# A fused window attention and GELU layer: identity and mask built on chip, first queries pre-scaled, and every engine's order written into the kernel

## The chip, the cores and the metric

The kernel runs on one core of one Trainium2 chip. A core has TensorE (PE; its weight loads are shown as PEld), VectorE (DVE), ScalarE (ACT), GpSimd (POOL) and SyncE (SP), each with its own stream of instructions in a fixed order; they meet at semaphores only. POOL and SP also issue DMAs. The metric is the device time of one execution in microseconds (us), lower is better.

## The reference

Streaming attention over 4 batches, 8 heads, 768 positions, 64 per head: each query sees the 128 latest keys and the first 4 ("sinks"). Its output, as 3072 tokens of 512, goes through two matrices with a quick GELU between them.

```python
scores = scale * np.matmul(q, k.transpose(0, 1, 3, 2))
rel = pos[:, None] - pos[None, :]
keep = is_sink | ((rel >= 0) & (rel < int(window)))
scores = np.where(keep, scores, -1000000000.0)
a = np.exp(scores - np.max(scores, axis=-1, keepdims=True))
a = a / (np.sum(a, axis=-1, keepdims=True) + 1e-09)
x = np.matmul(a, v)            # as tokens x 512
h = x @ w_in                   # 512 x 2048
g = h * (1.0 / (1.0 + np.exp(-1.702 * h)))
out = g @ w_out                # 2048 x 512
```

## The kernel before, in words

The 3072 tokens are 24 blocks of 128, six to a batch. `ORD` puts the first block of each batch (0, 6, 12, 18) at the front, since these see no earlier block; two blocks in this order make a group, 12 in all. The work of one block:

- POOL loads q, k and v in 16 bits (`load_block`, L369 and L378) into `qkn` and `v65`. Block 0's q and k come in 32 bits through the SP and ACT queues (L316) and are cast on chip (L374 to L376, recorded at the copy helper's L351).
- q and k are transposed to `qkT`: for the first 8 blocks in `ORD` on TensorE with an identity (`tq`, L471; copied out of PSUM at L347 or L351, the two lines of `copy` for VectorE and ScalarE), for the others by a DMA transpose on SP (L490).
- Scores: own block (`own`), the block before (`prv`), the sinks (`misc`), L524, L549 and L568; these matmuls use 64 of the array's 128 rows. For the four first blocks a mask is added by a matmul with a bf16 identity (`masks`, L516) before the scores; for the others VectorE picks own or previous scores by a predicate (L592).
- Softmax: VectorE takes maxima (L604), subtracts (L659), ScalarE takes the exponent (L692). For the first four blocks the second half goes straight through ScalarE with the negated, scaled maximum `nb` as bias (L635, L645).
- The weights are transposed, on TensorE for the first four blocks (`ta`, L755), by DMA for the others (L793), after which POOL's two selects split own and previous keys (L698, L704).
- Values (`av`, L814 to L824) with a column of ones for the sum, normalisation on VectorE (L835, L836) into `xn`, its transpose `xT` (L849 on TensorE for eight blocks, L862 by DMA).

A group then runs through the layer: eight units of `hT` (L884), the GELU on ScalarE into `gT` (L914), and two output tiles `o`, each in four pieces (L935), copied to `osb` and stored by SP (L953). The weights `w_in` and `w_out` come in four quarters each (L387, L396), in the same POOL queue as the blocks. Exponent and GELU need different tables on ScalarE.

What sets the order: the kernel first records its operations in a `Plan`, each with its engines, its cost, its dependences and the buffers it takes and gives. `Plan.run` then plays a list schedule over them with planned costs, in which every operation has a priority from the written list `KEYS`; where an operation may run on two engines, this decides which. The result is emitted as one fixed order per engine. `fill` matmuls (L975) that compute nothing are put where the plan sees TensorE idle in the first 45 us. `RING` gives the number of buffers of each kind: 3 PSUM banks `mm`, 2 `own`, 2 `pv`, 4 output tiles `osb`.

The loads at the start of SP are the lines L316 to L321: block 0's q, the identity, the mask `bias0`, then small constants.

Of the kernel before, what the change touches and what calls it, by code (L numbers as in the profile page):

```python
# [15 lines left out]
AF = mybir.ActivationFunctionType  # L16
# [15 lines left out]
    tq=(0, 1, 2, 3, 4, 5, 6, 7),  # L32
    ta=(0, 1, 2, 3),
    tx=(0, 1, 2, 3, 4, 5, 6, 7),
    nb={0: 1, 1: 1, 2: 1, 3: 1},
    wide=(1, 3),
    split=(0,),
    gbatch={},
    tanh=(),
    after0=25.0,  # L40
    vsb=15.0,
    slack={'v': 1.0, 's': 1.0, 'x': 1.0, 'e': 0.0, 'p': 0.0},
    merge=8,
    pemask=(0, 1, 2, 3),
    f32=(0,),
    sel2=(),
    fill=(1.5, 45.0, 0.15, 0.11),
    chain=99,
    gap=3,
    steady=8,  # L50
    after=8.0,
# [6 lines left out]
KEYS = [  # L58
    int(x)
    for x in """  # L60
# [32 lines left out]
""".split()  # L93
]
# [15 lines left out]
class Op:  # L110
    def __init__(self, eng, key, cost, emit, deps=(), take=(), give=(), table=None, lat=0.2, xfer=0.0, after=0.0, batch=0, post=0.0, slack=0.0, half=False):
        self.eng = eng if isinstance(eng, dict) else {eng: cost}
        self.key, self.emit = key, emit
        self.deps = [d for d in deps if d is not None]
        self.take, self.give, self.table, self.batch = list(take), list(give), table, batch
        self.lat, self.xfer, self.after, self.post, self.slack, self.half = lat, xfer, after, post, slack, half
        self.on = self.start = None
        self.end = self.done = 1.0e9
        for b in self.give:
            b.left += 1  # L120
# [6 lines left out]
class Plan:  # L127
    TABLE, LANES, ROWS = 1.35, 8, 0.1
    ENGINES = (PE, ACT, DVE, POOL, SP)

    PRE, SHARE = {POOL: 0.6, SP: 0.0}, {POOL: 0.68, SP: 0.32}

    def __init__(self, rings):
        self.ops, self.free, self.blk = [], dict(rings), 0
# [7 lines left out]
    def run(self):  # L142
        inf = 1.0e9
        t_eng = {e: 1.0 for e in self.ENGINES}
        free, table, batch, now, half = dict(self.free), "exp", 0, 0.0, False
        order, gives, events = [], [], [1.0]
        pending = {e: sorted((o for o in self.ops if e in o.eng), key=lambda o: (o.key, o.seq)) for e in self.ENGINES}
        events += [op.after for op in self.ops if op.after > 0.0]
        queue = {POOL: [], SP: []}
        lanes = {POOL: [], SP: []}  # L150
        count = len(self.ops)
        slacks = sorted({op.slack for op in self.ops if op.slack})

        def finish(op):
            events.append(op.done)
            for b in op.give:
                b.left -= 1
                b.t = max(getattr(b, "t", 0.0), op.done)
                if b.left == 0:
                    gives.append((b.t, b.ring))  # L160
                    events.append(b.t)

        while count or any(queue.values()):
            for item in [x for x in gives if x[0] <= now + EPS]:
                gives.remove(item)
                free[item[1]] += 1
            for e in self.ENGINES:
                if t_eng[e] > now + EPS:
                    continue
                for op in pending[e]:  # L170
                    if op.start is not None or op.after > now + EPS:
                        continue
                    if batch and op.table is not None and op.table != table:
                        continue
                    if any((d.end + 0.03 if d.on == e and not d.xfer else d.done + op.slack) > now + EPS for d in op.deps):
                        continue
                    if any(free[r] < n for r, n in op.need().items()):
                        continue
                    if op.xfer and len(lanes[e]) >= self.LANES and lanes[e][-self.LANES].done > now + EPS:
                        continue  # L180
                    break
                else:
                    continue
                cost = op.eng[e]
                if op.table is not None:
                    if op.table != table:
                        cost, table = cost + self.TABLE, op.table
# [824 lines left out]
```

## Time and profile before

| | |
|---|---|
| timed runs | 231.02, 232.11, 234.61 us (median 232.11) |
| profiled execution | 230.8 us |
| its span, first to last instruction | 229.1 us |
| granted TensorE clock | 0.999 |
| busy: TensorE, VectorE, ScalarE, POOL | 220.9, 132.4, 134.0, 110.8 us |
| fill matmuls | 65 of 2257 |
| first matmul that computes something | 5.66 us |
| first maximum on VectorE | 9.57 us |
| first matmul of the layer (hT) | 22.36 us |
| last matmul starts | 225.7 us |

The profile comes from one execution. Its times count from the start of the span. A row of the timeline gives start, busy time, engine, line, operation, output and inputs, the number of instructions, and in brackets the idle time of the engine before it and what ended that. A row of groups has the same names, then busy time and mean duration of one, then idle time before. In the table by windows, each stretch has its length and then the busy time of each engine with the number of its instructions, the granted clock, the DMA engines' share and GB/s. Matmuls overlap in the array, so their cost is the time from one start to the next, not the duration of one.

### The profile page before, as it was taken

How to read it: one execution, taken by the hardware profiler on the slowest of the kernel's cores; microseconds unless marked ns; L12 is line 12 of the kernel's file. 1: busy time of each engine (PE TensorE's matmuls, PEld its weight loads, DVE VectorE, ACT ScalarE, POOL GpSimd, SP SyncE). 2: the span in 40 equal slices, each digit the busy share in tenths (PEclk: the TensorE clock that was granted, in tenths of full speed). 3: DMA queues.
4: the chain of work that ended last, by engine and by line, in shares of the span. 5: the costliest groups of instructions: out<-in, count | busy, mean ns of one | idle time of the engine just before them, and what ended most of it. 6: DMA issues, size and time to landing. Idle time of an engine off the chain costs nothing.

```text
span 229.1 us, 5503 instructions
## 1 busy us (share of the span) xinstructions
PE 220.9 (96%) x2257; PEld 156.4 (68%) x2257; DVE 132.4 (58%) x331; ACT 134.0 (58%) x203; POOL 110.8 (48%) x122
## 2 busy tenths in 40 slices
PE   6998999999899999989999999999999999999994
PEld 3686986844686685676686686685596586685772
DVE  5499264887579177886793776676967830020000
ACT  4598765672766655548556757466467558451631
POOL 8982543906995196186294393397330240300000
PEclk9999999999999999999999999999999999999999
DMA  9999999999999999979999999999942922330202
GB/s 134 153 192 191 200 198 177 155 172 232 195 132 144 198 165 133 185 168 129 187 183 134 186 163 134 189 180 155 219 93 46 106 92 49 97 92 3 92 0 92
DMA packets 132280, 32.89 MB, mean 144 GB/s; under 512 B 124928, under 2 KB 129312, under 8 KB 132256
## 3 DMA queue, kind: packets, MB, share of 16 engines
q0 software_dynamic: 77024, 13.37, 76.3%
q1 hardware_dynamic: 54192, 18.92, 43.5%
q10 hardware_dynamic: 1040, 0.26, 0.5%
q8 instruction: 17, 0.28, 0.5%
q14 instruction: 7, 0.06, 0.1%
HBM read 27.43 MB, written 6.29 MB: 147 GB/s over the span
## 4 chain that ended last, share of the span: by engine, by line
PE 82%; DVE 9%; DMA 5%; issue 1%; ACT 1%; SPq 0%; DVEq 0%; ACTq 0%
PE o L935 34%; PE hT L884 33%; DMA xT<-xn 3%; PE av L820 2%; DVE mx L604 2%; PE own L549 2%; DMA bias<-cbias 2%; DVE xn L836 2%; PE av L824 2%; PE av L814 2%; DVE e L659 2%; PE tq L471 1%; PE prv L549 1%; PE misc L975 1%; DVE own L592 1%
## 5 line engine op out<-in xcount | busy, mean ns | idle before, releaser
L884 PE MATMUL hT<-xT,w_in 128*128 128x256 f16 (+1 forms) x832 | 92.8, 264 | 0.0
L935 PE MATMUL o<-w_out,gT 128*128 128x512 f16 (+1 forms) x400 | 89.9, 371 | 0.0
L914 ACT ACTIVATE gT<-hT 128x512 f16<-128x512 f32 x96 | 56.6, 597 | 45.4 <-PE hT L884 44.9
L884 PEld LDWEIGHTS <-w_in 128*128 128x128 f16 x832 | 74.3, 98 | 12.1 <-DMA xT<-xn 0.2
L935 PEld LDWEIGHTS <-gT 128*128 128x128 f16 x400 | 36.7, 98 | 35.0
L704 POOL TENSOR_SCALAR_AFFINE_SELECT atp<-at 128x1024 f16<-128x1024 f16 x20 | 21.9, 1094 | 71.7 <-DMA at<-a 67.5
L592 DVE COPY_PREDICATED own<-later,prv 128x512 f32<-128x512 uint16 x40 | 25.9, 692 | 25.7 <-PE prv L549 22.7
L604 DVE TENSOR_REDUCE mx<-own 128x4 f32<-128x512 f32 x48 | 30.9, 683 | 0.3 <-PE own L524 0.2
L692 ACT ACTIVATE a<-e 128x1056 f16<-128x1056 f32 (+1 forms) x24 | 23.8, 1007 | 11.3 <-issue 8.7
L659 DVE TENSOR_TENSOR e<-own,mx 128x512 f32<-128x512 f32 x44 | 28.8, 684 | 1.0
L351 ACT COPY osb<-o 128x512 f32<-128x512 f32 (+1 forms) x20 | 11.3, 565 | 25.3 <-PE o L935 20.0
L369 POOL DMA_DIRECT2D v<-in_v_dram x24 | 21.7, 912 | 5.1 <-DMA w_out<-in_moe_w_out_dram 3.3
L378 POOL DMA_DIRECT2D qkn<-in_q_dram x23 | 20.5, 905 | 5.2 <-DMA w_in<-in_moe_w_in_dram 3.1
L378 POOL DMA_DIRECT2D qkn<-in_k_dram x23 | 21.0, 914 | 3.2 <-DMA w_out<-in_moe_w_out_dram 2.1
L698 POOL TENSOR_SCALAR_AFFINE_SELECT at<-at 128x1024 f16<-128x1024 f16 x20 | 21.8, 1091 | 1.4
L835 DVE RECIPROCAL rcp<-av 128x4 f32<-128x4 f32 x48 | 8.4, 176 | 23.7 <-PE av L824 19.5
L836 DVE TENSOR_TENSOR xn<-av,rcp 128x256 f16<-128x256 f32 x48 | 20.4, 425 | 1.7
L820 PE MATMUL av<-v,at 128*128 128x65 f16 x192 | 17.1, 194 | 0.0
L820 PEld LDWEIGHTS <-at 128*128 128x128 f16 x192 | 14.2, 97 | 1.2 <-ACT at L351 0.2
L824 PE MATMUL av<-v,atp 128*128 128x65 f16 x160 | 14.8, 193 | 0.0
L914 ACT ACT_TABLE_LOAD x10 | 12.8, 1283 | 0.2
L975 PE MATMUL misc<-fill 128*128 128x256 f16 x65 | 11.1, 317 | 1.1 <-DVE fill L324 1.1
(56 smaller groups left out, 168.0 us busy)
## 6 DMA issues: line engine op xcount, KB each, us to landing
out_dram<-osb SPq DMA_DIRECT2D x23, 256.0 KB, 2.2
v<-in_v_dram POOLq DMA_DIRECT2D x24, 128.0 KB, 5.7
qkn<-in_k_dram POOLq DMA_DIRECT2D x23, 128.0 KB, 5.7
qkn<-in_q_dram POOLq DMA_DIRECT2D x23, 128.0 KB, 5.6
w_in<-in_moe_w_in_dram POOLq DMA_DIRECT2D x4, 512.0 KB, 10.3
w_out<-in_moe_w_out_dram POOLq DMA_DIRECT2D x4, 512.0 KB, 15.4
at<-a SPq DMA_TRANSPOSE x20, 4.2
rawk<-in_k_dram ACTq DMA_DIRECT2D x1, 256.0 KB, 4.5
```

Source lines behind the costliest of these rows:

```text
L378: key, 0.88, lambda: nc.gpsimd.dma_start(buf()[:, i, w], src), 0.9,
L592: nc.vector.copy_predicated(out=own[l](), mask=later.unsqueeze(1).to_broadcast((P, 4, P)), data=prv[l]())
L604: lambda l=l, own=own, small=small: nc.vector.tensor_reduce(out=small[:, l], in_=own[l](), axis=AX.X, op=ALU.max),
L659: nc.vector.tensor_tensor(out=e32()[:, 512 * l : 512 * l + 512].rearrange("p (j s) -> p j s", j=4), in0=own[l](), in1=small[:, l].unsqueez ...
L692: nc.scalar.activation(out=a16()[:, lo:hi], in_=e32()[:, lo:hi], func=AF.Exp, scale=scale)
L698: nc.gpsimd.affine_select(out=dst()[:, lo : lo + n], in_=at()[:, lo : lo + n], pattern=[[0, n], [1, P]], compare_op=ALU.is_ge, fill=0.0, b ...
L704: nc.gpsimd.affine_select(out=dst()[:, lo : lo + n], in_=at()[:, lo : lo + n], pattern=[[0, n], [-1, P]], compare_op=ALU.is_gt, fill=0.0, ...
L820: nc.tensor.matmul(av()[:, j], ato()[:, c], v65[:, b, h], start=(r == 0), stop=(r == 0))
L836: nc.vector.tensor_tensor(out=xn()[:, i].rearrange("p (j l) d -> p l j d", l=2)[:, l], in0=av()[:, :, 0:D], in1=rcp.unsqueeze(2).to_broadc ...
L884: nc.tensor.matmul(ht()[:, n], w_in16[:, c, bass.ts(f, P)], xt[g]()[:, tok, c], start=(c == 0), stop=(c == 3))
L914: lambda fs=fs, cols=cols, gt=gt, ht=ht: nc.scalar.activation(out=gt()[:, fs[0] : fs[-1] + 1, cols], in_=ht(), func=AF.Gelu_apprx_sigmoid),
L935: nc.tensor.matmul(po(), gt()[:, F, bass.ts(t, P)], w_out16[:, F, cols], start=(F == 0), stop=(F == NF - 1))
```

## The change

1. The identity and the mask `bias0` are no longer loaded. VectorE clears each, and one select on POOL writes the ones or the mask's value.
2. For the first block of each batch, the copy of the transposed q out of PSUM multiplies by the softmax scale, the maximum is written negated, and the `nb` operation is left out; the exponent then has factor 1 and the subtraction is an addition.
3. `Plan.run`, `KEYS` and the rule that places fills are removed. `ORDER` lists the operations in one written sequence with a letter for the engine of each (P, A, V, G, S), `FILL` the fills (45 in all) and `HOME` moves some PSUM tiles to a bank of another kind. The planned costs that are changed in the diff no longer decide anything.

```diff
-KEYS = [
-    int(x)
-    for x in """
-0 1 2 4 5 6 7 3 801 149 11 606 396 26 576 637 609 325 435 123 21 13 9 27 38 46 61 63 78 201 60 125 161 117 147 140
...
+ORDER = """
+9V 2V 18V 16V 4V 13V 19V 17V 12V 23G 0S 1S 7S 22G 28G 29G 3G 15V 11V 26G 21A 20V 108P 109V 110P 5G 10V 113P 27G 132P
+133A 111V 112V 114P 130P 116V 32G 24G 25G 36G 37G 131A 118A 115V 31G 117V 174P 135P 136P 137V 119A 122P 175A 176P
+139V 120P 138V 121V 152P 177A 154P 179P 33G 180P 123V 153A 141A 142P 155A 140A 35G 157P 182V 181V 184A 30G 41G 40G
...
+FILL = dict(
+    map(int, x.split(":"))
     for x in """
+108:16 110:2 174:7 154:3 144:11 164:4 128:2
...
+HOME = dict(x.split(":") for x in "0:own 2:pv 6:own 8:own 10:pv 12:own 16:own 17:own 19:pv 20:pv 22:mm 25:own 26:own 27:mm 28:mm 29:own 32:pv 35:pv 38:own 39:pv 41:pv 43:own 45:own 46:mm 49:mm 50:mm 52:mm 53:mm 54:own 56:pv 57:mm 59:own 60:mm 61:mm 62:mm 64:own 66:mm 67:own 69:own 70:mm 168:own 170:pv 173:pv 174:own 177:pv 178:pv 179:pv 181:own 183:own 185:pv 187:pv 188:pv 191:pv 192:own 195:pv 197:pv 203:pv 204:own".split())
...
     def ps(tag, shape, dt, name):
-        return Buf(tag, lambda: psp.tile(list(shape), dt, tag=tag, bufs=RING[tag], name=name))
+        buf = Buf(tag, lambda: psp.tile(list(shape), dt, tag=buf.ring, bufs=RING[buf.ring], name=name))
+        plan.bufs.append(buf)
+        return buf
...
-    o_ident = hw(-2000, 0.4, lambda: nc.sync.dma_start(ident, ident_d.ap()), 0.1)
-    o_bias0 = hw(-1999, 0.4, lambda: nc.sync.dma_start(bias0, bias0_d.ap()), 0.1)
+    z_i = plan.add(DVE, -2003, 0.1, lambda: nc.vector.memset(ident, 0.0))
+    o_ident = plan.add(
+        POOL, -2003, 0.35,
+        lambda: nc.gpsimd.affine_select(
+            out=ident, in_=ident, pattern=[[-1, P]], compare_op=ALU.not_equal, fill=1.0, base=0, channel_multiplier=1
+        ),
+        deps=[z_i],
+    )
+    z_b = plan.add(DVE, -2002, 0.1, lambda: nc.vector.memset(bias0, 0.0))
+    o_bias0 = plan.add(
+        POOL, -2002, 0.35,
+        lambda: nc.gpsimd.affine_select(
+            out=bias0[:, 4:P], in_=bias0[:, 4:P], pattern=[[-1, P - 4]], compare_op=ALU.is_ge, fill=NEG, base=-4,
+            channel_multiplier=1,
+        ),
+        deps=[z_b],
+    )
...
-                        lambda e, b=b, w=w, tp=tp: copy(e, qk_of(b)[:, 4 * w : 4 * w + 4], tp()[:, 4 * w : 4 * w + 4]),
+                        lambda e, b=b, w=w, tp=tp, f=scale if w == r == 0 else 1.0: copy(
+                            e, qk_of(b)[:, 4 * w : 4 * w + 4], tp()[:, 4 * w : 4 * w + 4], f
+                        ),
...
-                        out=small[:, l], in_=own[l](), axis=AX.X, op=ALU.max
+                        out=small[:, l], in_=own[l](), axis=AX.X, op=ALU.max, negate=r == 0
...
-        if nb:
+        nbias, o_nb = small, top
+        if nb and r > 0:
...
+        factor = scale if r > 0 else 1.0
...
-                            scale=scale, bias=nbias[:, l, j : j + 1],
+                            scale=factor, bias=nbias[:, l, j : j + 1],
...
-                    op=ALU.subtract,
+                    op=ALU.subtract if r > 0 else ALU.add,
...
-    order = plan.run()
...
+    for n, ring in HOME.items():
+        plan.bufs[int(n)].ring = ring
+    engines = dict(P=PE, A=ACT, V=DVE, G=POOL, S=SP)
     with tc.manual_schedule():
-        for op in order:
-            for n in range(idle.get(op, 0)):
+        for item in ORDER:
+            op = plan.ops[int(item[:-1])]
+            for n in range(FILL.get(op.seq, 0)):
                 nc.tensor.matmul(misc[:, 256:512], fill[:, 0:P], fill, start=True, stop=True)
-            op.emit(op.on) if len(op.eng) > 1 else op.emit()
+            op.emit(engines[item[-1]]) if op.many else op.emit()
```

What the new order does on the engines around the start and in the queues: on TensorE 16 fills come before block 0's first transposes, 29 after them and before the first `hT`; block 0's mask comes after both its transposes. On VectorE the first operations are clears, then the cast of block 0's q (on ScalarE before), the scaled copy, the bf16 identity, the copy of k. On POOL the order is: four loads (k and q of block 6, q and k of block 18), the identity's select, q of 12, the mask's select, k of 12, v of 18, 0 and 6, q and k of 1, v of 12, three quarters of `w_in`, k and q of 2, the last of `w_in`, q and k of 3 and 4, then the four quarters of `w_out`; two of the four `vsb` products also go to POOL. On SP some output stores stand far behind the tile's copy: those of the tiles 3_1, 4_1, 5_1 and 7_0 (group, half) are the 43rd, 59th, 51st and 60th of 69 entries.

More of the change, by code (lines that the diff above doesn't have):

```diff
@@ L31 @@
 CFG = dict(
[L32 to L51, printed above, removed]
+    tq=(0, 1, 2, 3, 4, 5, 6, 7), ta=(0, 1, 2, 3), tx=tuple(range(8)), nb={0: 1, 1: 1, 2: 1, 3: 1}, wide=(1, 3),
+    split=(0,), gbatch={}, tanh=(), after0=25.0, vsb=15.0, slack=dict(v=1.0, s=1.0, x=1.0, e=0.0, p=0.0), merge=8, pemask=(0, 1, 2, 3), f32=(0,), sel2=(), fill=(1.5, 45.0, 0.15, 0.11), chain=99, gap=3, steady=8, after=8.0,
     loads="q0 k0 q6 k6 v0 v6 q12 k12 q18 k18 i0 v12 v18 i1 i2 i3 q1 k1 o0 o1 q2 k2 o2 o3 v1 v2".split(),
@@ L127 @@
 class Plan:
-    TABLE, LANES, ROWS = 1.35, 8, 0.1
-    ENGINES = (PE, ACT, DVE, POOL, SP)
-    PRE, SHARE = {POOL: 0.6, SP: 0.0}, {POOL: 0.68, SP: 0.32}
     def __init__(self, rings):
-        self.ops, self.free, self.blk = [], dict(rings), 0
+        self.ops, self.bufs, self.free, self.blk = [], [], dict(rings), 0
     def add(self, *a, **kw):
@@ L140, in add @@
         return op
[L142 to L187, printed above, removed]
-                    if op.table == "gate":
-                        batch = (batch or op.batch) - 1
-                if e == PE and op.half != half:
-                    cost, half = cost + self.ROWS, op.half
-                op.on, op.start, op.end = e, now, now + cost
-                t_eng[e] = op.end
-                if op.xfer:
-                    events.append(op.end + self.PRE[e])
-                events += [op.end] + ([] if op.xfer else [op.end + op.lat + x for x in slacks])
-                for r, n in op.need().items():
-                    free[r] -= n
-                for b in op.take:
-                    b.taken = True
-                if op.xfer:
-                    queue[e].append([op, op.xfer])
-                    lanes[e].append(op)
-                else:
-                    op.done = op.end + op.lat
-                    finish(op)
-                pending[e] = [o for o in pending[e] if o.start is None]
-                order.append(op)
-                count -= 1
-            live = {e: q[0] for e, q in queue.items() if q and q[0][0].end + self.PRE[e] <= now + EPS}
-            rate = {e: self.SHARE[e] if len(live) > 1 else 1.0 for e in live}
-            events = [t for t in events if t > now]
-            step = min(events + [now + h[1] / rate[e] for e, h in live.items()], default=inf) - now
-            assert step < inf, [(e, [(o.seq, o.key) for o in p[:5]]) for e, p in pending.items()]
-            now += step
-            for e, h in live.items():
-                h[1] -= step * rate[e]
-                if h[1] <= EPS:
-                    queue[e].pop(0)
-                    h[0].done = now + h[0].post
-                    events += [h[0].done + x for x in slacks]
-                    finish(h[0])
-        self.span = max(op.done for op in order)
-        return order
@@ L230, in _consts @@
     later = j > p
-    bias0 = np.where(later & (j >= 4), NEG, 0.0).astype(ml_dtypes.bfloat16)
     bias1 = np.where(later[:, :4], NEG, 0.0).astype(ml_dtypes.bfloat16)
@@ L306, with hw @@
     plan.blk = -1
-    def hw(key, cost, fn, xfer, **kw):
-        return plan.add(SP, key, cost, fn, xfer=xfer, post=1.3, **kw)
+    def hw(key, cost, fn, xfer, late=0.0, **kw):
+        return plan.add(SP, key, cost, fn, xfer=xfer, post=1.3 + late, **kw)
     raw, o_raw = {}, {}
@@ L327 @@
     o_identb = plan.add(
-        DVE, -91, 0.1, lambda: nc.vector.tensor_copy(out=identb, in_=ident), deps=[o_ident]
+        DVE, -2001, 0.15, lambda: nc.vector.tensor_copy(out=identb, in_=ident), deps=[o_ident]
     )
     z_k = plan.add(DVE, -90, 0.2, lambda: nc.vector.memset(ksb, 0.0))
-    z_v = plan.add(DVE, -89, 2.4, lambda: nc.vector.memset(vsb, 0.0))
-    z_1 = plan.add(DVE, -88, 0.3, lambda: nc.vector.memset(v65[:, :, :, D:D1], 1.0))
+    z_v = plan.add(DVE, -89, 1.8, lambda: nc.vector.memset(vsb, 0.0))
+    z_1 = plan.add(DVE, -92, 0.25, lambda: nc.vector.memset(v65[:, :, :, D:D1], 1.0))
     z_n = plan.add(DVE, -60, 0.1, lambda: nc.vector.memset(neg, NEG))
@@ L475 @@
                 a = plan.add(
-                    PE, K0 - 48 + w, 0.45 if n < 2 and not CFG["fill"] else 0.27, lambda w=w, f=t_qk: f(w), deps=[ld["qk"[w] + str(b)], o_ident],
+                    PE, K0 - 48 + w, 0.23, lambda w=w, f=t_qk: f(w), deps=[ld["qk"[w] + str(b)], o_ident],
                     take=[tp], give=[qkn[g]],
@@ L532 @@
             s_msk = plan.add(
-                PE, K0 - 41, 0.9 if n == 0 and not CFG["fill"] else 0.43, lambda own=own, f=masks: f(own), deps=[o_bias0, o_identb] + (o_qkt[b] if n else []), take=own,
+                PE, K0 - 41, 0.43, lambda own=own, f=masks: f(own), deps=[o_bias0, o_identb] + (o_qkt[b] if n else []), take=own,
                 slack=slack["s"],
@@ L536 @@
         s_own = None if both else plan.add(
-            PE, K0 - 40, 0.5 if n < 2 and not CFG["fill"] else 0.24, lambda b=b, own=own, f=scores: f(own, b),
+            PE, K0 - 40, 0.235, lambda b=b, own=own, f=scores: f(own, b),
             deps=o_qkt[b] + [s_msk], take=[] if s_msk else own, give=[home[b]], slack=slack["s"] if s_msk is None else 0.0,
@@ L568, in sinks @@
                     nc.tensor.matmul(snk()[:, j], qk_of(b)[:, j], ksb[:, bb, j], start=True, stop=True)
-            s_snk = o_snk[b] = plan.add(PE, K0 - 40, 0.15, sinks, deps=([s_own] if n >= CFG['steady'] else []) + o_qkt[b] + [o_ks[bb]], take=[snk], give=[home[b]], slack=slack["s"])
+            s_snk = o_snk[b] = plan.add(PE, K0 - 40, 0.115, sinks, deps=([s_own] if n >= CFG['steady'] else []) + o_qkt[b] + [o_ks[bb]], take=[snk], give=[home[b]], slack=slack["s"])
         e32 = sb("e32", (P, 8 * P + 32), FP32, f"e32_{b}")
@@ L651 @@
                     plan.add(
-                        ACT, K0 - 36.5, 1.14, exps, deps=[o_nb, z_a[n % RING["a16"]]],
+                        ACT, K0 - 36.5, 1.14, exps, deps=[o_nb if r > 0 else mx[l], z_a[n % RING["a16"]]],
                         take=[a16], give=[own[l]], table="exp",
@@ L667 @@
                 plan.add(
-                    DVE, K0 - 38.7, 0.6, sub, deps=[top, mx[l]], take=[e32], give=[own[l]]
+                    DVE, K0 - 38.7, 0.6, sub, deps=[top if r > 0 else None, mx[l]], take=[e32], give=[own[l]]
                 )
@@ L955 @@
                 )
-    if KEYS:
-        for op, key in zip(plan.ops, KEYS):
-            op.key = key
-    order = plan.run()
-    idle, last = {}, 1.0
-    if CFG["fill"]:
-        lo, hi, rest, one = CFG["fill"]
-        for op in order:
-            if op.on == PE:
-                a, z = max(last, lo), min(op.start, hi)
-                for b in o_snk:
-                    if o_snk[b].start < z and o_sub[b].done + 0.5 > a:
-                        a = max(a, min(z, o_sub[b].done + 0.5))
-                idle[op] = max(0, int((z - a - rest) / (one if a > 6.0 else 2 * one)))
-                last = op.end
+    for n, ring in HOME.items():
+        plan.bufs[int(n)].ring = ring
+    engines = dict(P=PE, A=ACT, V=DVE, G=POOL, S=SP)
     with tc.manual_schedule():
-        for op in order:
-            for n in range(idle.get(op, 0)):
+        for item in ORDER:
+            op = plan.ops[int(item[:-1])]
+            for n in range(FILL.get(op.seq, 0)):
                 nc.tensor.matmul(misc[:, 256:512], fill[:, 0:P], fill, start=True, stop=True)
-            op.emit(op.on) if len(op.eng) > 1 else op.emit()
+            op.emit(engines[item[-1]]) if op.many else op.emit()
 _INS = ['q', 'k', 'v', 'n_sink', 'window', 'moe_w_in', 'moe_w_out']
```

64 lines of the change are left out of this document (49 added, 15 removed), and 31 rows, old and new, of the table KEYS.

## Prediction

> **What bounds the kernel now.** I read the page first (shares of the span), then the table by windows, then the timeline of the start, then TensorE's waits and the DMA landings.
>
> ```profile
> span 229.1 us, 5503 instructions
> PE 220.9 (96%) x2257; PEld 156.4 (68%) x2257; DVE 132.4 (58%) x331; ACT 134.0 (58%) x203; POOL 110.8 (48%) x122
> L975 PE MATMUL misc<-fill 128*128 128x256 f16 x65 | 11.1, 317 | 1.1 <-DVE fill L324 1.1
> ```
>
> TensorE is the bound, but 65 of its matmuls (L975) compute nothing. Laid end to end at their common start-to-start pace (hT 0.109 us per 128x256, o 0.216 per 128x512, 0.056 per 128x128, 0.029 per 65 columns), all the others make 203.5 us. The last starts at 225.7 and 3.4 us of eviction and store follow. So 225.7 - 203.5 = 22.2 us is fill and waiting. Counted the same way by stretch, 15.2 of it lies before 22.3 us, 2.0 between 22.3 and 56.7, 4.9 between 56.7 and 180, 0.1 after.
>
> ```profile
> 10.30:22.30 12.00, 11.08 (x140) 8.72 (x139) 11.46 (x29) 10.73 (x32) 7.37 (x10) 1.00 1.77 187
> 56.70:180.00 123.30, 121.94 (x1307) 85.71 (x1306) 87.01 (x215) 76.38 (x100) 70.11 (x73) 1.00 1.36 158
> 180.00:229.10 49.10, 45.99 (x374) 32.19 (x370) 6.44 (x22) 22.31 (x36) 6.50 (x6) 1.00 0.23 66
> ```
>
> The columns after the length are PE, PEld, DVE, ACT, POOL. In the first line VectorE is busy 11.46 of 12 us: the start-up is VectorE's chain (maxima, subtractions, copies, normalisations of blocks 0, 6, 12, 18), and TensorE's 11.08 is padded with fills. From 56.7 on TensorE is full, and from 180 nothing else matters.
>
> ```profile
> 4.62 0.62 ACT L351 CAST qkn<-rawq 128x512 f16<-128x512 f32 x1 [2.03 <-DMA rawq<-in_q_dram]
> 5.32 0.62 ACT L351 CAST qkn<-rawk 128x512 f16<-128x512 f32 x1
> 5.66 0.59 PE L471 MATMUL tq<-ident,qkn 128*128 128x128 f16 x4 [1.15 <-DMA ident<-cident]
> 6.49 1.01 PE L516 MATMUL own<-bias,identb 128*128 128x512 bf16 x2 [0.24 <-DMA bias<-cbias]
> 9.57 1.29 DVE L604 TENSOR_REDUCE mx<-own 128x4 f32<-128x512 f32 x2 [0.23 <-PE own L524]
> ```
>
> The first real matmul waits for the identity's DMA, the mask matmul for the mask's, and block 0's k transposes (7.29) stand behind the mask in TensorE's order. VectorE starts its chain at 9.57.
>
> **The change, part by part.** I measure a landmark by its lag: its time less the work queued ahead of it on TensorE. The first matmul of hT1 starts at 33.5 with 18.4 us of work ahead, a lag of 15.1.
>
> *Identity and mask.* Two DMAs leave SP. Their replacement stands on POOL after the fourth load issue, which ended at 4.97. The nearest row is the 128x1024 select at 1.09 us; an eighth of the columns gives 0.14, so each costs 0.14 to 1.09, and I take 0.2 (proportion, plus a little for the start). Identity at 5.2. The q cast moves to VectorE behind its memsets (before they ended at 4.85, now two more at 0.11 and one at 0.17 fewer: 4.9); a copy is 0.41 to 0.69 there, taken 0.45, so 5.35. Transposes of q 5.4 to 5.85 (4 at 0.107), copy 0.42, bf16 identity 0.23: 6.5. Meanwhile the k cast ends at 5.94, transposes 6.0 to 6.4, copy to 6.9, masks (2 at 0.43) to 7.35, block 6's k transposes to 7.8, scores 0.4 to 8.2. First maximum at 8.25, not 9.57. Behind the two selects POOL's later loads issue 0.4 later; they land 5.6 after issue, at 10.9 and 12.1.
>
> The Trainium skill, "SBUF — State Buffer", section "Who interferes with whom", says a copy or cast in a two-port mode on VectorE and a GpSimd operation block each other for the whole instruction. That speaks against this change, since the q cast and the identity's select now fall together; the first maximum would then be some 0.4 later and the estimate below 228.3. No row here shows such a pair; the 1.79 us memset at 1.45 left the load issues beside it at 0.9 to 1.0.
>
> *Negated maximum, scaled queries.* The four L635 scalings (0.16 each on VectorE) go; three q copies on ScalarE become activations and one on VectorE a multiply, of the same 128x512 form, which I cost as the copies (0.59, 0.42). 0.6 us leaves VectorE's chain; the order counts below already omit it.
>
> *The order, start-up.* Block 6's q lands at 8.04, its transposes end at 8.65, its copy on ScalarE at 9.3. TensorE then has 7 fills at the early pace (0.213, as until 10.3) to 10.1, block 18's transposes, masks, and block 6's scores end near 11.0: VectorE waits from 10.05 to 11.0. From there its order holds 6 maxima and 3 subtractions at 0.60, 6 copies at 0.34 and 8 normalisations at 0.55 = 11.84, with 0.2 for a wait on ScalarE: 23.05. Then block 12's transposes and two hT units of 0.9: hT1 starts at 25.55 with 13.2 us of work ahead. Lag 12.35, so **-2.7**.
>
> *The weights.* POOL now issues 12 block loads ahead of the first w_in, and 6 more before w_out. By the landing steps of before (0.95 a block load, w_in 2.04 to 3.43, mean 2.54, w_out mean 2.67) the w_in quarters land at 20.2, 22.8, 25.3, 29.6 and the first needed w_out at 38.5. Their users stand at 21.0, 23.75, 29.1, 30.9 and 27.0 + 12.35 = 39.4. Hidden, with 0.9 to spare: 0.
>
> *The order, steady part.* TensorE switches between whole and half array 48 times, not 52. Around a visit the next o group takes 0.97 instead of 0.86 and about 0.07 goes on the way in: two visits fewer, **-0.3**. Blocks 2, 3, 4 have 2 to 3 us more work between scores and values (18.3, 16.3, 19.1 against 16.5, 13.5, 16.4), which covers the 1.1 us lost between 56.7 and 61.1, **-1.1**. Block 7 has 12.7 instead of 17.2. Its path: packs, maxima, sinks and subtractions 4.3, exponent 1.08, DMA transpose 4.2 (median, up to 5.9), two selects 2.2 = 11.8 with nothing ahead in any queue, 13.8 with one slow transpose: 0 to 2 us, I take the middle, **+1.0**. Two of the vsb products go to POOL (0.73 on VectorE), where selects have long waits beside them: 0. The tail (last eviction 0.37, store 2.2) is the same.
>
> Sum: 230.8 for the profiled execution (span 229.1) - 2.7 - 0.3 - 1.1 + 1.0 = 227.7. The timed runs are 231.0, 232.1 and 234.6; the nearest lies 0.2 above, so 227.9.
>
> **The rivals.**
>
> *More falls away.* If the array is at full pace by 9, the 7 fills and the masks shrink and VectorE's wait of 0.95 closes; if block 7 meets no slow transpose, 1.0 goes too; and if half of the other 1.9 us of real waits after 61 goes: 227.9 - 2.9 = 225.0. For: the pace did change inside this stretch (0.213 at 10.08, 0.113 at 10.29). Against: the order has no spare work before block 6's scores.
>
> *The weights come late.* With each w_in at 3.43 and w_out at 3.01, the first w_out lands 4.3 later, at 42.8; TensorE stands 3.4 us at its first o and the gain is eaten: 231.3. For: 3.43 happened once. Against: it happened once in four.
>
> *The array slows.* Twenty fills are gone, all before the first hT. If TensorE falls back to the pace of 0.213 for want of work, it needs as long as at the start, 9.2 us (1.1 to 10.3), to leave it, and loses half of that: 227.9 + 4.6 = 232.5. Against: the longest hole in the new start is below 1.5 us, as before (1.15). The Trainium skill, "TensorE: Matmul & The Clock Gate", says the array falls to half rate after an idle window of about 3.4 us; by that rule this doesn't happen. The granted clock column shows 1.00 throughout, also where the pace is half, so the pace is what to read.
>
> *Slower: stores behind transposes.* The new SP order holds four finished output tiles (3_1, 4_1, 5_1, 7_0) back, two of them to the 59th and 60th of 69 entries, while only four osb buffers exist. The stores that free the others then stand behind transposes: two of at and one of qkT ahead of 3_1's and 6_0's, 1.44 + 1.44 + 2.50 = 5.4 us of issue. An output tile takes 3.5 us of TensorE, so from an SP delay of 3.5 on, the eviction waits for a buffer, o for PSUM: 1.9 each, four times, 227.9 + 7.6 = 235.5. Against: SP mostly waits for others (70 us on L953 alone).
>
> **How the numbers follow.** Forecast 0.42 (own range 226.0 to 229.8: identity late by 0.8, block 7 at 0 or 2, weights on time), more falls away 0.28, weights late 0.10, slow array 0.05, stores 0.15. 224.4 to 233.2 leaves out most of the stores (0.13) and the end of the first rival (0.05). A measurement here tells about 2%: faster means below 227.5 (0.98 x 232.11). That is the first rival and a third of the forecast: 0.41. Slower, above 236.7, is the stores' case with a little more than its price: 0.10. The rest, 0.49, is within.
>
> **What would show it.** First tq at 5.4 and no DMA behind it; first maximum near 8.25; hT1 near 25.5; VectorE near full from 11 to 23; first o near 39.4 without a wait on w_out; av2 near 53.3; waits at block 7's values under 2 us; no o or copy waiting for a store. A first maximum after 9, a w_out wait, or an eviction released by an output DMA makes it wrong.

## The result, and the profile after

| | before | changed |
|---|---|---|
| median of 16 runs | 232.00 us | 229.87 us |
| ratio | | 0.9928 (95%: 0.9906 to 0.9951) |
| span of the profiled execution | 229.1 | 227.8 |
| last matmul starts | 225.7 | 224.3 |

Some 1.7 us are won by the ratio (0.72% of 232), 2.1 by the medians of the table and 1.3 between the two profiled executions; forecast were 4.2 against the median and 3.1 against the profiled execution. The table's medians are over all executions; the ratios, and all medians further down, leave out those that ran in the chip's slower state. The start of the changed kernel, in the timeline:

```profile
4.79 0.43 DVE L267 CAST qkn<-rawq 128x512 f16<-128x512 f32 x1
...
5.03 0.33 POOL L225 TENSOR_SCALAR_AFFINE_SELECT ident<-ident 128x128 f16<-128x128 f16 x1
...
5.41 0.38 PE L391 MATMUL tq<-ident,qkn 128*128 128x128 f16 x4 [0.90 <-POOL ident L225]
...
6.60 0.59 PE L438 MATMUL own<-bias,identb 128*128 128x512 bf16 x2
...
7.81 1.29 DVE L526 TENSOR_REDUCE mx<-own 128x4 f32<-128x512 f32 x2 [0.26 <-PE own L446]
```

The transposes wait for POOL's select and for no DMA, the mask stands behind block 0's q and k transposes, and VectorE starts at 7.81 instead of 9.57. The stretches of the prediction, in the table by windows:

```profile
10.30:22.30 12.00, 10.40 (x158) 8.15 (x157) 11.21 (x29) 10.85 (x27) 9.73 (x12) 1.00 1.94 177
56.70:180.00 123.30, 121.62 (x1267) 84.40 (x1266) 84.81 (x206) 74.38 (x102) 73.60 (x78) 1.00 1.32 157
180.00:227.80 47.80, 44.57 (x376) 31.87 (x373) 9.88 (x27) 19.77 (x32) 5.09 (x5) 1.00 0.26 74
```

They tell little apart. The page's chain of work that ended last does (first before, then changed):

```profile
PE 82%; DVE 9%; DMA 5%; issue 1%; ACT 1%; SPq 0%; DVEq 0%; ACTq 0%
```

```profile
PE 62%; DMA 16%; POOL 11%; issue 6%; DVE 1%; ACT 1%; POOLq 0%; SPq 0%
```

VectorE, 9% of the old chain, has 1% of the new one; DMAs and POOL have come in. Where the time went shows when TensorE's starts are taken apart: each matmul that computes something counts with the common start-to-start pace of its kind, the rest of a stretch is fills and waiting (us). The levels hang on the paces taken and on where the count starts (the prediction's sum up to 22.2, these to 20.8); the differences change by less than 0.1 with them.

| stretch | before | changed | difference |
|---|---|---|---|
| to 22.3 | 14.18 | 11.46 | -2.72 |
| 22.3 to 45 | 1.14 | 0.61 | -0.53 |
| 45 to 61 | 1.46 | 2.78 | **+1.32** |
| 61 to 80 | 0.56 | 0.34 | -0.22 |
| 80 to 100 | 1.50 | 2.29 | **+0.79** |
| 100 to the end | 1.95 | 1.89 | -0.06 |
| sum | | | -1.42 |

At 53 us the changed kernel is 3.67 us of work ahead; at 61 it is 1.93 ahead, at 100 1.36. TensorE's longest waits in the changed kernel:

```profile
PE av L738 <- DVE vsb L346: 1.8, 1, 1.8
...
PE hT L808 <- DMA xT<-xn: 0.9, 1, 0.9
...
PE av L744 <- POOL at L622: 0.7, 2, 0.5
```

The first stands at 54.94, in front of av2. The instructions that it hangs on, VectorE's and POOL's (timeline):

```profile
53.40 1.49 DVE L346 TENSOR_TENSOR vsb<-vsa,ownm 32x520 f16<-32x520 f32 x1 [3.25 <-DMA vsa<-in_v_dram]
```

```profile
50.41 1.09 POOL L628 TENSOR_SCALAR_AFFINE_SELECT atp<-at 128x1024 f16<-128x1024 f16 x1 [8.78 <-DMA at<-a]
51.57 1.09 POOL L622 TENSOR_SCALAR_AFFINE_SELECT at<-at 128x1024 f16<-128x1024 f16 x1
53.25 1.09 POOL L628 TENSOR_SCALAR_AFFINE_SELECT atp<-at 128x1024 f16<-128x1024 f16 x1 [0.58 <-DMA at<-a]
54.41 1.43 POOL L622 TENSOR_SCALAR_AFFINE_SELECT at<-at 128x1024 f16<-128x1024 f16 x1
```

Two things are late here: `vsa`, the sinks' values, whose load the new order puts on SP behind the transposes of at2 and at1 (issued at 48.12, before at 3.83), and these transposes themselves, for which POOL stood idle for 8.78 us. The groups of the three transposes (count, then issue min/median/max; last line: time to landing) before and changed:

```profile
L793 SPq DMA_TRANSPOSE at<-a x3: 1300/1421/2363, 48.3 to 52.3; - x3
...
DMA to landing us min/median/max: 3.3/3.9/4.5
```

```profile
L717 SPq DMA_TRANSPOSE at<-a x3: 1526/1999/4266, 42.2 to 48.9; - x3
...
DMA to landing us min/median/max: 5.2/8.2/9.4
```

at2 and at1, the first two, start 6 us earlier and land 1 to 2 us earlier (at1 at 53.19 against 54.35). In the old order five loads of POOL's queue were still to land when the first transpose was issued, and they ran out beside the first two (the last landed at 52.08, before the third was issued); in the new one eight are still to land, and they run until 53.00 beside all three.

### The profile page after: what moved, and what is told of

Same layout as the page of the kernel before. It is cut to its first block, busy times and chain, and to the rows that moved or that the text cites. A ratio compares the mean times of both kernels' runs of the same rounds, so it can differ in the third digit from the quotient of the medians.

```text
span 227.8 us, 5439 instructions
## 1 busy us (share of the span) xinstructions
PE 216.8 (95%) x2237; PEld 153.0 (67%) x2237; DVE 136.0 (60%) x334; ACT 127.3 (56%) x196; POOL 114.3 (50%) x126
## 4 chain that ended last, share of the span: by engine, by line
PE 62%; DMA 16%; POOL 11%; issue 6%; DVE 1%; ACT 1%; POOLq 0%; SPq 0%
PE hT L808 28%; PE o L859 25%; DMA w_out<-in_moe_w_out_dram 6%; DMA w_in<-in_moe_w_in_dram 5%; POOL qkn L298 3%; DMA xT<-xn 3%; DMA at<-a 3%; POOL at L622 3%; POOL atp L628 2%; POOL v L289 2%; PE own L471 2%; PE av L744 2%; PE av L748 2%; PE av L738 1%; PE prv L471 1%
## 5 line engine op out<-in xcount | busy, mean ns | idle before, releaser
L859 PE MATMUL o<-w_out,gT 128*128 128x512 f16 (+1 forms) x400 | 91.0, 371 | 0.0
L838 ACT ACTIVATE gT<-hT 128x512 f16<-128x512 f32 x96 | 54.7, 599 | 49.4 <-PE hT L808 49.0
L514 DVE COPY_PREDICATED own<-later,prv 128x512 f32<-128x512 uint16 x40 | 26.5, 692 | 30.8 <-PE prv L471 25.9
L526 DVE TENSOR_REDUCE mx<-own 128x4 f32<-128x512 f32 x48 | 31.7, 685 | 1.6 <-PE own L446 1.1
L622 POOL TENSOR_SCALAR_AFFINE_SELECT at<-at 128x1024 f16<-128x1024 f16 x20 | 22.2, 1110 | 1.4
L298 POOL DMA_DIRECT2D qkn<-in_k_dram x23 | 20.8, 906 | 1.7 <-POOLq L906 0.8
L271 ACT COPY osb<-o 128x512 f32<-128x512 f32 (+1 forms) x18 | 10.0, 560 | 19.4 <-PE o L859 18.9
L267 DVE COPY osb<-o 128x512 f32<-128x512 f32 x7 | 4.8, 690 | 19.8 <-PE o L859 19.5
## 6 DMA issues: line engine op xcount, KB each, us to landing
w_out<-in_moe_w_out_dram POOLq DMA_DIRECT2D x4, 512.0 KB, 12.6
```

Of the source, the lines that this page charges most:

```text
L298: key, 0.88, lambda: nc.gpsimd.dma_start(buf()[:, i, w], src), 0.9,
L514: nc.vector.copy_predicated(out=own[l](), mask=later.unsqueeze(1).to_broadcast((P, 4, P)), data=prv[l]())
L526: lambda l=l, own=own, small=small, r=r: nc.vector.tensor_reduce(out=small[:, l], in_=own[l](), axis=AX.X, op=ALU.max, negate=r == 0),
L622: nc.gpsimd.affine_select(out=dst()[:, lo : lo + n], in_=at()[:, lo : lo + n], pattern=[[0, n], [1, P]], compare_op=ALU.is_ge, fill=0.0, b ...
L838: lambda fs=fs, cols=cols, gt=gt, ht=ht: nc.scalar.activation(out=gt()[:, fs[0] : fs[-1] + 1, cols], in_=ht(), func=AF.Gelu_apprx_sigmoid),
L859: nc.tensor.matmul(po(), gt()[:, F, bass.ts(t, P)], w_out16[:, F, cols], start=(F == 0), stop=(F == NF - 1))
```

## The experiments

The theories after these traces: T1, the loads and the transposes beside them make a wall near 53 us; T2, the misplaced `vsa` load is the wait; T3, as a consequence of either, the start-up's gain is lost again at that place. In the expectations, blocks 4 to 9 of the loads and exponents are counted by their place in `ORD`: 4, 5, 6 are at1, at2, at3, and 8 and 9 are the two blocks of qkT4. Ratios are to the kernel before, timed beside the runs on the same chip. From e9 on that kernel itself spread from 230.8 to 234.5 us, so kernels are set there against the changed kernel timed beside them (e12 and e16). e9 to e15 keep e1's move. Numbers in `ORDER` are shown for one engine alone.

**e1, the sinks' load early** (SP)

```diff
-... 8S 101S 236S 212S 100S 260S 292S ...
+... 8S 100S 101S 236S 212S 260S 292S ...
```

> One load moved in SP's order: the sink values of the first batch (vsa) go out before the transposes of block 1 and 2 (at1, at2) instead of behind them. In the changed kernel vsb waited 3.2 us for this load and ran 1.49 us beside POOL's selects, and TensorE waited 1.92 us at 54.94 for it. T2 (the misplaced load is the wait): av2 starts at about 53.2, the wait before it is under 0.3 us, the time falls by 1.6 to 1.9 us, to about 228.1 (ratio to the kernel before 0.985). T1 (the loads of POOL's queue and the transposes beside them set a wall, at1's select ends at 55.8 whatever is done): the wait of 1.92 turns up again in front of av1, the time falls by 0.0 to 0.35 us, to 229.5 to 229.9 (ratio 0.991 to 0.993).

Ratio 0.995 (0.9932 to 0.9968), 230.25 us: no gain. T2 by itself falls. `vsb` is now done at 51.9, in 0.68 us, and av2 doesn't wait, but the wait stands one block further on, in TensorE's timeline:

```profile
56.42 0.20 PE L743 MATMUL av<-v,at 128*128 128x65 f16 x1 [1.25 <-POOL at L621]
```

**e2, the same with one w_out quarter less**

```diff
-42G 43G 52G 55G ...
+42G 52G 55G ...
-w_out16[:, F, cols]    ... ld_wout[n]
+w_out16[:, F % 12, cols]    ... ld_wout[n % 3]
```

> As the run before, and the fourth quarter of w_out is not loaded (its columns are multiplied by the first quarter instead, so that part of the output is of the wrong weights): 512 KB less in POOL's queue, some 2.6 us of it. T1 (wall of loads): the v loads and at1's transpose land 2 to 2.6 us earlier, at1's select ends about 53.3, and the time falls by 1.9 us or more against the changed kernel, and by 1.5 or more against the run with the sink values moved alone. T2: nothing beyond the run with the sink values moved alone, within 0.3 us.

Ratio 0.9796 (0.9757 to 0.9836), 226.51 us: 3.7 us below e1. The transposes and the chain:

```profile
L716 SPq DMA_TRANSPOSE at<-a x3: 1315/2009/2020, 42.2 to 46.5; - x3
...
DMA to landing us min/median/max: 3.5/4.1/5.3
```

```profile
PE 87%; DVE 4%; DMA 2%; ACT 2%; POOL 2%; SPq 1%; issue 1%; POOLq 0%; ACTq 0%
```

The first two are issued about when they were in the changed kernel, and the three land in half the time (median 4.1 against 8.2). The waits at 82.65 and 92.40 are gone too: fills and waiting fall to 0.36 between 45 and 61 and 0.52 between 80 and 100. T1 holds, and reaches further than I expected.

**e3, one load more**

```diff
+            if f == 3:
+                nc.gpsimd.dma_start(spare, moe_w_out[bass.ts(f, 512), :].rearrange("(c p) f -> p c f", p=P))
```

> The changed kernel with one more load of 512 KB in POOL's queue behind w_out's four (into a tile that nothing reads). T1 (wall of loads): v2, v1 and the transposes beside them land 2.0 to 2.6 us later, av2 and av1 too, and the time rises by 2.0 to 2.6 us, to about 232. T2 (only SP's order counts): the sink values' load is not in that queue, so av2 starts where it did and the time rises by less than 0.4 us.

231.52 us, ratio 1.002 (0.9985 to 1.0055): 1.65 us more than the changed kernel by the medians and 2.1 by the ratios, near T1's figure and far above T2's. In its trace at1 lands at 56.88 and the wait before av2 is 4.36; that execution was one of the longest (233.8 us), for the reason told under e12.

**e4, constants by DMA again**

```diff
-0S 1S 7S ... 3G ... 5G
+0S 1S 3S 5S 7S ...        (memsets and selects out)
```

> The changed kernel with identity and mask loaded by DMA on SP again, right behind the first queries and keys; the order, the scaled queries and the negated maximum stay. First tq about 0.9 to 1.3 us later, and the first maximum with it. T3 (the start-up's gain is taken back at the wait near 55 us, T1 or T2 alike): the wait of 1.92 shrinks by the same 0.9 to 1.3, and the time rises by 0 to 0.3 us. Rival (what is won in the start-up is kept to the end): the time rises by 0.9 to 1.3 us, to about 231.

229.72 us, ratio 0.9938 (0.9917 to 0.9958): within 0.2 us of the changed kernel. First tq at 6.03 and first maximum at 9.06; TensorE is 1.17 us of work behind the changed kernel at 22.3 and 0.8 ahead of it at 61. T3 holds: a start that is later by this much costs no time. Not all of the 1.17 is the constants': after a hole of 1.64 us in front of its first tq the array ran at half pace from 7.4 to 10.7, and e16, the changed kernel at half pace, is 1.05 behind as well.

**e5, the new operations in the old order**

```diff
-ORDER = (the new list), FILL 45, HOME
+ORDER = (what the old plan gave), FILL 65, no HOME
```

> The changed operations (identity and mask made on chip, first queries scaled on their way out of PSUM, maximum negated) in the order of the kernel before. Theory of the loads (what bounds the time from about 45 us on is when the last value load and the transposes at2, at1 land, not the start-up): the operations alone win some 1 us of start-up and keep at most half of it, ratio to the kernel before 0.995 to 1.000. Rival (the operations carry the whole gain and the searched order none): ratio 0.993, as the changed kernel.

Ratio 0.9976 (0.9917 to 1.0035): unclear, since the interval holds both. What the operations are worth without the new order stays open.

**e6, at7 before qkT5** (SP)

```diff
-... 328S 321S ...
+... 321S 328S ...
```

> The changed kernel with one swap on SP: at7's transpose goes out before qkT5's, whose issue held SP from 71.67 to 75.55. If the wait of 0.66 at 82.65 in front of av7's values is SP's order alone, at7 lands 3 to 4 us earlier, that wait goes, and the time falls by 0.4 to 1.0 us, to about 229.1. If it is the traffic of the loads (q and k land one after another until 76.2 beside at5's transpose), at7's issue only waits for its input or the queue instead, and what at7 wins qkT5 loses: 0 to +0.5 us.

Ratio 0.9971 (0.9922 to 1.002): no gain over the changed kernel's 0.9928 to be seen, as the second reading had it, though the interval holds a small one. No trace of it is read here.

**e7, the kernel before with one load less**

```diff
+            if f == 3:
+                nc.gpsimd.dma_start(spare, moe_w_out[bass.ds(f * 512, P), 0:8])
+                return
-w_out16[:, F, cols]
+w_out16[:, F % 12, cols]
```

> The kernel before, its plan unchanged, with the fourth quarter of w_out not loaded (four columns' worth of bytes are; its part of the output is made with the first quarter instead). In the changed kernel taking that load away won 3.6 us. Theory of the loads: the kernel before is late from its start-up and hardly waits for loads, so here it wins 0.0 to 1.2 us, to 230.4 to 231.6 (ratio 0.995 to 1.000), and without that load the change would have been worth the 3 to 4 us forecast. Rival (the loads bound both kernels alike, and the change gained elsewhere): it wins 3 us or more here too, to 228.5 (ratio 0.987).

231.00 us, ratio 0.9965 (0.9942 to 0.9988): the load is worth about 0.8 us here and 3.4 to 3.7 in the changed kernel (229.87 and e1's 230.25, less 226.51). So the loads bound the new order and hardly the old one. Without that load the change, with e1's move, gains some 3.9 us by the ratios (0.9965 less 0.9796, of 232); the medians differ by 4.5, but were taken on two chips.

**e8, values first** (POOL, and e1's move)

```diff
-42G 43G 52G 55G 53G 105G 48G 56G 45G 44G 237G 213G 261G
+42G 43G 48G 45G 44G 52G 55G 53G 105G 56G 237G 213G 261G
```

> The changed kernel with the sinks' load early and, in POOL's queue, the last three value loads ahead of the four loads of queries and keys of blocks 8 and 9 that stood before them: the same bytes in another order. If the wait at av1 is for the value load itself, that load lands about 3 us earlier and the time falls by 1.0 to 1.9 us, to about 228.5. If all of the transfers share the DMA engines (the transposes land when the loads are through, whichever load is last), at1 still lands near 53 and the time changes by less than 0.4 us, or rises where qkT4 now waits for its queries.

229.78 us, by median as the changed kernel's 229.87; the ratio, 0.9882 (0.9827 to 0.9936), stands against a kernel before that spread from 231.1 to 233.2. The trace decides: the value loads land by 46.3, at1 still lands at 52.76, and av1 waits:

```profile
55.31 0.20 PE L743 MATMUL av<-v,at 128*128 128x65 f16 x1 [1.12 <-POOL at L621]
```

It isn't one load that is late; the transposes are, for the transfers beside them.

**e9, e10, e11: two loads behind at2's selects** (POOL; e11 also SP)

```diff
 e9, against e8
-... 52G 55G 53G 105G 56G 237G 213G 261G
+... 52G 55G 105G 237G 53G 56G 213G 261G
 e10
+... 45G 44G 52G 55G 53G 105G 237G 56G 48G 213G 261G
 e11: e10, and
-... 260S 292S 635S 284S ...
+... 260S 635S 284S 292S ...
```

> The order with the values first, and besides it two of the four loads of queries and keys of blocks 8 and 9 issued by POOL only behind at2's selects: nothing is left out, 256 KB of it move from before the wall near 53 us to behind it. If the transposes wait for the DMA engines: at2 lands near 48.5 and at1 near 50.5 instead of 50.34 and 53.19, at1's selects end near 55 (two issues of 0.9 us stand between the selects), the waits at av2 and av1 fall from 2.5 to under 0.8 us, and the time falls by 0.8 to 1.7 us against the changed kernel, unless qkT4 comes late. If instead the transposes are slow by themselves: no change, or up to 1.8 us slower for the issues between the selects.

> As the run before, with one load of queries or keys and the value load of block 6 (needed from about 57 us on) issued behind at2's selects in the place of two loads of queries and keys. Same theory, less to lose at qkT4: 0.8 to 1.9 us faster than the changed kernel, about 228.3. Rival (slow transposes): 0 to 1.8 us slower.

> The run before, with the transpose of block 7's probabilities (and one store) ahead of qkT4's on SP, since qkT4 now waits for its last load. If qkT4's late load holds SP in the run before, block 7's transpose lands earlier and the time falls by up to 0.5 us against it; if not, the same within 0.3 us, or slower by what qkT4 loses.

> The changed kernel itself, as the reference for the three others in the same call: 229.1 to 230.5 us, ratio to the kernel before 0.990 to 0.995, and again a wait of 1.5 to 3 us in front of av2's first value product.

Medians 236.27, 232.43 and 235.72 against 230.47 for the changed kernel again (ratios 1.0104, 0.9983, 1.0151, each within 0.007, and 0.9844): all slower, so the expectations' sums were wrong. Their first half was right, e9's transposes landing at 48.25, 49.30 and 50.58. The second half is in POOL's timeline of e9, and in TensorE's:

```profile
49.48 1.09 POOL L621 TENSOR_SCALAR_AFFINE_SELECT at<-at 128x1024 f16<-128x1024 f16 x1
50.52 1.82 POOL L297 DMA_DIRECT2D qkn<-in_k_dram  x2
52.33 1.11 POOL L627 TENSOR_SCALAR_AFFINE_SELECT atp<-at 128x1024 f16<-128x1024 f16 x1
```

```profile
59.85 0.23 PE L470 MATMUL own<-qkT 64*128 64x128 f16 x2 [2.34 <-DMA qkT<-qkn]
```

The two issues hold at1's selects, and the keys come so late that the next scores wait 2.34. e11 makes that wait longer, not shorter (5.02, against 2.09 in e10).

I had overlooked a second cost. Behind such waits the array falls to half pace: the granted clock is 0.50 for 3.4 us, which is 1.7 us of work where TensorE is busy all that time. The traces show it once in e9 (72.1 to 75.4) and e10 (62.3 to 65.6) and twice in a row in e11 (62.4 to 69.2) and in e3 (57.0 to 63.9). The changed kernel is not safe from it. In e12 it waited 2.74 before av2, where its first profile had 1.75, and the array slowed behind that (TensorE's timeline, then the table by windows):

```profile
55.91 0.27 PE L738 MATMUL av<-vsb,at 128*128 128x260 f16 x1 [2.74 <-DVE vsb L346]
```

```profile
50.00:56.00 6.00, 3.26 (x16) 1.44 (x15) 1.59 (x3) 2.16 (x3) 3.90 (x4) 1.00 1.35 155
56.05:59.40 3.35, 3.35 (x39) 2.54 (x38) 1.97 (x8) 0.00 (x0) 3.28 (x4) 0.51 1.03 278
```

In the two profiles that the table of stretches compares, the clock is 1.00 up to 180 us, so the +1.32 holds none of this.

**e13, e14, e15: two loads behind an exponent** (POOL idles there)

```diff
+            if item == "53G":      # e15: "56G"; e14: plan.ops[211]
+                nc.gpsimd.tensor_copy(gate, plan.ops[259].take[0]()[:, 0:8])
 e13
+42G 43G 48G 45G 44G 52G 55G 105G 53G 56G 237G 213G 261G
 e15
+42G 43G 45G 44G 52G 55G 53G 105G 56G 48G 237G 213G 261G
```

> Values first, sinks early, and two of the loads of queries and keys of blocks 8 and 9 held back by a copy of 8 columns on POOL that reads block 6's exponent, so POOL issues them near 45 us in its idle time, not between its selects. If the place behind earlier loads makes the transposes late: at2 lands near 48.5 and at1 near 50, at1's selects end near 53, no wait over 0.4 us before av2 or av1, qkT4 no later than in the changed kernel, and the time falls by 1.5 to 2.5 us against the changed kernel of the same call. If the total counts: at1 still lands at 52 or later, the time changes by under 0.5 us.

> As the run before with the copy reading block 4's exponent, some 1.5 us earlier, so the two loads start beside at2's and at1's transposes. Place: between the changed kernel and the run before, 0.5 to 2 us faster than the changed kernel. Total: under 0.5 us.

> As the run with block 6's exponent, but one load of queries or keys and the value load of block 6 are held back. Place: 1.5 to 2.5 us faster than the changed kernel, av3's values land in time (needed from 57 us). Total: under 0.5 us.

> The changed kernel itself as the reference of this call: 229.1 to 231 us, a wait of 1.5 to 3 us in front of av2.

Medians 229.93, 230.37 and **228.35** against 230.35; ratios 0.9926 (0.9901 to 0.9951), 0.9925 (0.9884 to 0.9966), **0.9841 (0.9795 to 0.9888)** and 0.9944 (0.9917 to 0.9970). e15 beats both kernels, with nothing left out; its POOL and its transposes:

```profile
44.85 0.19 POOL L888 COPY gate<-a 128x8 f16<-128x8 f16 x1 [6.81 <-ACT a L615]
45.08 0.94 POOL L297 DMA_DIRECT2D qkn<-in_k_dram  x1
46.02 0.88 POOL L288 DMA_DIRECT2D v<-in_v_dram  x1
48.81 1.09 POOL L627 TENSOR_SCALAR_AFFINE_SELECT atp<-at 128x1024 f16<-128x1024 f16 x1 [1.91 <-DMA at<-a]
```

```profile
L716 SPq DMA_TRANSPOSE at<-a x3: 1316/1914/3292, 42.3 to 47.8; - x3
...
DMA to landing us min/median/max: 4.9/6.5/7.5
```

at2 lands at 48.74 and at1 at 51.90, 1.6 and 1.3 us before those of the changed kernel's first profile, and the time falls by 2. Two more executions of the changed kernel had them at 50.86 and 54.16 (e12) and at 50.88 and 52.02 (e16), so at2 is early beyond that spread and at1 hardly. No wait before av2 or av1 is left in its trace, where the three of the changed kernel lost 1.75, 2.74 and 0.76. The place among the transfers counts here, and not only their total. But e13, with another pair of loads held back, gains at most 0.4, and e14 nothing. In e13's trace at1 landed at 53.41 beside the two loads, in an execution that had already waited 1.04 at 27.75 for a load of keys; in e14's it landed at 55.21. Why the one pair helps and the other doesn't is not settled. In e15 the waits between 80 and 100 us are still 2.80, so there is more to be had.

## Why the prediction was wrong

- **Start-up, -2.7: right in size, in part by luck.** 2.72 measured. First tq 5.41 (5.4 expected), first o 39.22 (39.4), lag at hT1 12.6 (12.35). The first maximum came at 7.81 instead of 8.25, since the array was at full pace from 5.4. That is the execution's luck: e16, the same kernel, kept half pace there (four transposes 0.58 instead of 0.38), had its first maximum at 8.98 and 1.05 us less work done at 22.3. The kernel before was profiled at half pace up to 10.3, so at like pace only some 1.7 of the 2.72 are the change's. The lag of 15.1 before is also some 0.8 too small, beside the prediction's own 15.2 of fills and waiting up to 22.3 and 0.7 more up to 33.5 in the same trace.
- **Where the lead goes (T3).** At 61 the changed kernel's first profile and e16 both stood at 45.0 us of work, though e16 had started 1.05 behind: a later start met a shorter wait. That place isn't fixed, though. e12 started like the first profile and stood 1.9 lower at 61, by its longer wait and the half pace behind it; e16 did not wait before av2 at all, but 0.76 before av1.
- **Port lock between the q cast and the identity's select, 0 taken: right.** Cast 0.43 and select 0.33 overlap, and neither is stretched. Where VectorE's instruction has two inputs in SBUF it was otherwise: `vsb` took 1.49 beside POOL's selects and 0.68 alone (e1). The Trainium skill, "SBUF — State Buffer", section "Who interferes with whom", says that such an instruction contends with a GpSimd one that reads SBUF; these rows agree.
- **Identity and mask, 0.14 to 1.09 each, 0.2 taken:** 0.33 and 0.31.
- **Weights, 0: right.** No o waits for w_out in this profile. But I asked only whether the weights land in time for their own users, and not for what they hold up.
- **Two visits less, -0.3:** not seen; from 100 on the two kernels differ by 0.06.
- **"Blocks 2, 3, 4 have 2 to 3 us more work between scores and values ... which covers the 1.1 us lost", -1.1: this step failed.** It came out as +1.32. I measured the distance in TensorE's work alone, and did not ask when the DMA transpose in between would land; where I priced one, for block 7, I took what it took before (4.2 median). Issued 6 us earlier, it runs beside the loads, and takes 8.2. By the same step the 18 block loads that I had counted ahead of the weights should have been followed to where the queue ends, 53.0. e2 takes the wait away with a load, e7 shows that the old order hardly had it. The sinks' load, which I overlooked on SP, was a second wait in the shadow of the first (e1).
- **Block 7, +1.0: 0.79, near it by luck.** Two waits are new, 0.66 at av7 and 1.11 at the next group's xT, and two of before are gone, 0.43 and 0.57 at 99 us. The place is half right. Both new waits hang on the loads (gone in e2); SP's order alone won nothing that could be seen (e6).
- **Rivals.** The profile shows no wait for a late weight, no slow array and no eviction behind a store. The case that came is none of them: transposes that slow down beside loads. The page's DMA row, at 9 tenths in nearly every slice up to 150 us (first before, then changed), could have warned that a transfer moved earlier would find the DMA engines busy:

```profile
DMA  9999999999999999979999999999942922330202
```

```profile
DMA  9999999999999999999999999998982703620302
```

- **The slow array** did come in other executions, e12 of the changed kernel among them. The rule that the prediction takes from the Trainium skill, "TensorE: Matmul & The Clock Gate", half rate after an idle window of about 3.4 us, does not agree with these traces as a bound: a wait of 2.74 was enough (e12), one of 1.75 was not (the first profile).

The Trainium skill, "DMA: Bandwidth & Descriptors", section "Queues, rings and completion order", says that each DMA engine takes packets in turn from the queues that have work. That fits: SP's transposes neither stood behind POOL's loads nor passed them, but took about twice as long (8.2 against 3.9 before and 4.1 in e2) while these lasted.

## What to carry to other kernels

A gain at the start is worth what the next wait leaves of it. Before counting a lead to the end, follow each queue to the landing of its last transfer ahead of the next join, and price a DMA by what will run beside it at its new time, not by its old duration. When a wait is named, take it away alone: here another stood right behind it, and the remedy was neither the load that the profile named nor a later issue on a busy POOL, but two loads held back into POOL's idle time, and only one of the three such arrangements helped. Where runs are this close, read more than one execution: the same kernel waited 1.75, 2.74 and not at all before the same matmul.

## What the runs showed of the hardware

- The DMA transpose of nine 128x128 pieces (`at`) took 3.3 to 4.5 us from issue to landing where the loads ran out beside it (before), 5.2 to 9.4 in their midst; its issue held SP for up to 4.27 us instead of 1.3.
- The select of 128x128 took 0.33 us, a third of that of 128x1024 (1.09): not in proportion.
- TensorE's pace in the first 11 us differed between executions of one kernel by a factor of two (a transpose of 128x128 every 0.055 or every 0.107 us, in the changed kernel's first profile and in e16), with a granted clock of 1.00 shown for both.
- A fall to half pace later on is shown by that clock: 0.50 for 3.4 us at a time behind waits of TensorE (e12 behind 2.74 us; e4 from 7.4 us on, after 1.64), and it costs up to 1.7 us each time.
